# Turning the cluster codes of a routing attention: a TensorE product or a VectorE block transpose

## The chip, the cores and the metric

The kernel runs on one core of one Trainium2 chip. The metric is the device time of one execution in microseconds (us). The core has five engines that work side by side, each through its own list of instructions in order: TensorE (PE; its weight loads are shown as PEld), VectorE (DVE), ScalarE (ACT), GpSimd (POOL) and SyncE (SP). SP computes nothing here: it issues nearly all transfers between the on-chip memory (SBUF) and the device memory (DRAM), and it too works in order, so that a transfer which must wait for something holds up every transfer listed behind it.

## The reference

The first half is an attention in which a query sees only the keys of its own cluster. The second half is a two-layer feed-forward block.

```python
B, H, S, D = 4, 8, 768, 64          # 16 clusters per head
q_assign = argmax(einsum('bhsd,hcd->bhsc', q_n, c_n), -1)   # cluster of each query
k_assign = argmax(einsum('bhsd,hcd->bhsc', k_n, c_n), -1)   # cluster of each key
mask   = q_assign[:, :, :, None] == k_assign[:, :, None, :]
scores = where(mask, q @ k.T / sqrt(D), -1e9)
attn   = softmax(scores);  out = attn @ v
x = out.transpose(0, 2, 1, 3).reshape(B * S, H * D)        # 3072 x 512
h = x @ w_in                                                # 512 x 2048
y = (h - tanh(h)) @ w_out                                   # 2048 x 512
```

## The kernel before

The work is cut into 16 pairs: pair n is one batch and two heads, whose 2 x 64 dimensions fill the 128 partitions. The queries of a pair are taken in two halves of 384, and the keys in six chunks of 128. One step `(n, half, s)` treats two key chunks, so a half has three steps and there are 96 steps in all; the first batch (pairs 0 to 3) takes all its first halves first. A loop over the steps (L1238) lays down the instructions of all engines in the order in which they are to run: nothing is rearranged afterwards.

A step does this. TensorE multiplies keys and queries (`begin`, L499), ScalarE takes the exponential (L521), and VectorE multiplies it by the mask (`select`, L531). The mask is made there too: VectorE compares a row of query codes with the code of the key in its partition. TensorE then multiplies the values with the result (`value`, L556). For the first halves of pairs 1 to 3 (`masked`) the mask is instead a second TensorE product of one-hot codes that is added to the scores (L510), with the tile `hot` from which `one_hot` (L474 and L478) makes them.

The codes come from `similar` (TensorE, L376), `turn_back`, `route` and `route_on` (VectorE, L386 to L414). They end in the tile `code`, one token per partition and 24 columns per pair (two sides, two heads, six chunks). The query codes must also be had along a row, the same row in all partitions. That is what `publish` and the functions behind it do: `publish` (L425) turns the 12 columns of the query side (24 columns, both sides, for masked pairs) into 12 or 24 rows of 128 codes and stores them in DRAM as `q_codes`, a row of 256 bytes (B) from each partition. `spread` (L442) or `spread_both` (L459) reads them back into all partitions, as `row` or `hot`. The reading transfer waits until the storing one has landed. `publish(0)` and `publish(1)` stand in the opening, before the loop; those of pairs 2 and 3 run two steps after their `similar`; from pair 4 on `publish` is two steps after `route_on` and well ahead of the first use.

TensorE writes into PSUM, and most short-lived results (`pq` of `publish`, `sim`, `den`, `tally`, `h`, `o`, `pu` and `pd`) take turns in a pool `ps_f` of three buffers. A new one waits until the one three places earlier has been read.

Between the steps the feed-forward work of the batch before is laid down as filling for TensorE: `plain_items` (L730, L746) for half of the first batch, and a scheme with fewer products, one level of Strassen's method, for the rest (`up_product`, L933, and `down_product`, L1038). The combined weights for it are made once: VectorE's `made` (L831), stored to `up_factors` and `down_factors` (L795, L814), and read back piece by piece as `stream` (L853). `publish(4)` falls into the time in which they are made. VectorE meets `den` (L707) and `made` there, behind `publish` in its list.

The denominators of the softmax make a detour over DRAM of their own: `invert` and `compact` store a small tile with `back` (L659, L668), 128 partitions of 48 or 24 B, and read it back (L680, L685).

Of the kernel before, what the change touches and what calls it, by code (L numbers as in the profile page):

```python
# [30 lines left out]
F32 = mybir.dt.float32  # L31
BF16 = mybir.dt.bfloat16
# [7 lines left out]
P = 128  # L40
# [18 lines left out]
def kernel(  # L59
# [10 lines left out]
    nc = tc.nc  # L70
# [13 lines left out]
    HCH = NCH // 2  # L84
# [8 lines left out]
    const = ctx.enter_context(tc.tile_pool(name="const", bufs=1))  # L93
    dram = ctx.enter_context(tc.tile_pool(name="dram", bufs=6, space=DRAM))

    ident = const.tile([P, P], F32, name="ident")
# [9 lines left out]
    each = const.tile([P, 2 * (B * (HP - 1) - 1), 2 * TB // P], F32, name="each")  # L106
    other = const.tile([P, 2 * TB // P], F32, name="other")
    flag = const.tile([1, 1], I32, name="flag")

    out_r = out.rearrange("(b j p) m -> b j p m", p=P, j=NCH)  # L110

# [67 lines left out]
    def fast():  # L179
# [3 lines left out]
        rtp = cx.enter_context(tc.tile_pool(name="rtp", bufs=1))  # L183
# [7 lines left out]
        ps_f = cx.enter_context(tc.tile_pool(name="ps_f", bufs=3, space=PSUM))  # L191
# [38 lines left out]
        def constants():  # L230
            nc.vector.memset(inverses, 0.0)
            make_identity(nc, ident)
            nc.vector.memset(ones, 1.0 / words)
            nc.vector.memset(wholes, 0.0)

            mine_first = const.tile([P, 1], F32, name="mine_first")
            nc.vector.tensor_reduce(
                out=mine_first, in_=ident.rearrange("p (a b) -> p a b", b=D // 2)[:, :, 0], axis=AX.X,
                op=ALU.add,
            )  # L240
            nc.vector.tensor_copy(out=firsts, in_=mine_first.to_broadcast([P, D]))
            for c in range(C):
                nc.vector.memset(down[:, c : c + 1], float(C - c))

            spread_ = const.tile([P, 2, D], F32, name="spread_")
            nc.vector.memset(spread_, 0.0)
            nc.vector.tensor_copy(
                out=spread_[:, :, 0:C], in_=down.unsqueeze(1).to_broadcast([P, 2, C])
            )
            spread_ = spread_.rearrange("p a c -> p (a c)")  # L250
            nc.vector.tensor_tensor(out=spread_, in0=spread_, in1=ident, op=ALU.mult)
            nc.vector.reduce_sum(out=mine_code, in_=spread_, axis=AX.X)
# [54 lines left out]
        raw_qk, vals, turned, codes, q_codes = {}, {}, {}, {}, {}  # L307
        pairs = [(b, p) for b in range(B) for p in range(HP)]

        BL = 32  # L310
# [109 lines left out]
        def masked(n: int, half: int):  # L420


            return summed(n, half) and n > 0

        def publish(n: int):  # L425

            sides = 2 if masked(n, 0) else 1
            G = HCH * 4 * sides
            ps = ps_f.tile([G, P], F32, name="pq", tag="f")
            code = codes[n] if sides == 2 else codes[n][:, 0]  # L430
            code = code.rearrange("p a b c -> p (a b c)" if sides == 2 else "p j h -> p (j h)")
            nc.tensor.transpose(out=ps, in_=code, identity=ident)
            t = rtp.tile([G, P], BF16, name=f"qc{sides}")
            nc.vector.tensor_copy(out=t, in_=ps)
            shape = [2, HCH, 2, P] if sides == 1 else [2, sides, 2, HCH, P]
            q_codes[n] = dram.tile(shape, BF16, name=f"q_codes{sides}")
            order = "a j h p -> (a j h) p" if sides == 1 else "h i a j p -> (h i a j) p"
            nc.sync.dma_start(q_codes[n].rearrange(order), t)

        rows, hots = {}, {}  # L440

# [651 lines left out]
        def before(n: int):  # L1093


            def turns():
                turn(n, 1, nc.scalar)
                if rowwise(n):
                    turn(n, 0, nc.scalar)

            yield turns
            if n < HP:
                yield lambda: similar(n)
            else:
                yield None
            yield lambda: (turn_back(n), route(n), route_on(n))
            yield lambda: publish(n)
            if masked(n, 0):
                yield lambda: spread_both(n)
                yield lambda: one_hot(n)  # L1110
# [29 lines left out]
        for n in range(1, HP):  # L1140
            b, p = pairs[n]
# [35 lines left out]
        centroid_load()  # L1177
        load(0)
        constants()
        keep_warm(7)  # L1180
        centroid_norms()
# [15 lines left out]
        turn(1, 1, nc.scalar)  # L1197
        keep_warm(3)
        publish(0)
        load(2, (0,))  # L1200
        spread(0, 0)
# [12 lines left out]
        round_piece(rounding.pop(0))  # L1214
        begin(steps[1])
        publish(1)
        select(*steps[0][:2], 0)
        spread_both(1)
# [19 lines left out]
        for at, (n, half, s) in enumerate(steps):  # L1238
            b, p = pairs[n]
# [177 lines left out]
        for t, bound in (  # L1417
# [7 lines left out]
            out=fits, in0=inverse, scalar1=MOST_INVERSE * words, scalar2=None, op0=ALU.is_le  # L1425
        )
        nc.vector.scalar_tensor_tensor(
            out=fits, in0=inverse, scalar=words / SUM_MOST, in1=fits, op0=ALU.is_ge, op1=ALU.mult
        )
        checks = [fits, largest]  # L1430
        if words == 2:
            nc.vector.tensor_scalar(
                out=smallest, in0=smallest, scalar1=HIGH_LEAST, scalar2=None, op0=ALU.is_ge
# [198 lines left out]
```

## Time and profile before

| what | us |
|---|---|
| median of 3 runs (956.2 to 957.47) | 956.89 |
| the profiled execution | 955.51 |
| its span in the profile | 953.6 |
| TensorE busy in the span | 939.2 (98%) |
| VectorE busy | 580.3 (61%) |
| GpSimd busy | 510.5 (54%) |
| ScalarE busy | 293.5 (31%) |
| share of the chain of waits on TensorE | 89% |
| `pq` product (L432), 16 of them, each | 0.275 |
| copy of `pq` to `qc` (L434), 16 of them, each | 0.275 |

The span runs from the first to the last instruction of the profile; the time of an execution has another 1.9 us around it. "Busy" of TensorE is modelled for pipelined products, whose durations overlap: the distance from one start to the next says what a product costs, not its duration. The chain of waits follows the end of the kernel back, at each instruction to what released it. Where a table gives an idle time and a releaser, an instruction that waits for several things is put down to the last of them.

### The profile page before, as it was taken

Reading aid. Unit: us, or ns where it says so; the run is one execution under the profiler, and the core shown is the slowest. Engines: PE = TensorE matmul, PEld = TensorE weight load, DVE = VectorE, ACT = ScalarE, POOL = GpSimd, SP = SyncE. Lnnn points to the kernel's source line nnn. Section 1 sums busy time; section 2 is a strip of 40 time slices with the busy share of each in tenths; the row PEclk is TensorE's granted clock in tenths of the full one; section 3 lists DMA queues with packets and bytes.
Section 4 is the critical chain, followed back from the end, with each engine's and each line's share of the span. In section 5 each row is a group of like instructions: output and inputs, shape, how many; then the busy total and the mean of one; then the engine's idle time right before and its main releaser. Section 6 shows DMA issues by size and latency. Waiting matters only on the chain.

```text
span 953.6 us, 16953 instructions
## 1 busy us (share of the span) xinstructions
PE 939.2 (98%) x6584; PEld 469.0 (49%) x6584; DVE 580.3 (61%) x1111; ACT 293.5 (31%) x453; POOL 510.5 (54%) x364
## 2 busy tenths in 40 slices
PE   8999999999999999999999999999999999999997
PEld 5434443355653334444465665444456665445664
DVE  6647686976776678566845567766656338443011
ACT  5586564223332332323322112333331220222000
POOL 1026353456775465777785453867797343657500
PEclk9999999999999999999999999999999999999999
DMA  7767465892736645474565645557334223323331
GB/s 193 205 182 154 118 172 128 249 278 86 196 116 160 158 136 132 151 180 132 170 170 182 153 152 187 126 184 170 114 128 147 98 84 100 116 78 132 107 106 37
DMA packets 166764, 139.85 MB, mean 147 GB/s; under 512 B 116580, under 2 KB 145044, under 8 KB 163988
## 3 DMA queue, kind: packets, MB, share of 16 engines
q1 hardware_dynamic: 160292, 117.15, 44.7%
q0 software_dynamic: 6240, 21.50, 6.9%
q8 instruction: 54, 0.88, 0.4%
q14 instruction: 34, 0.28, 0.1%
q10 hardware_dynamic: 144, 0.03, 0.0%
HBM read 117.48 MB, written 21.17 MB: 145 GB/s over the span
## 4 chain that ended last, share of the span: by engine, by line
PE 89%; DVE 3%; DMA 2%; ACT 1%; issue 1%; SPq 0%; DVEq 0%; ACTq 0%
PE pu L933 26%; PE pd L1038 22%; PE sc L499 13%; PE av L556 13%; PE o L746 6%; PE h L730 4%; PE sim L376 1%; PE den L617 1%; DVE e L531 1%; DMA stream<-up_factors 1%; PE den L571 1%; DVE diff L899 1%; PE den L590 1%; DVE den L707 1%; DMA row<-q_codes 0%
## 5 line engine op out<-in xcount | busy, mean ns | idle before, releaser
L547 POOL TENSOR_TENSOR sum<-sum,e 128x768 f32<-128x768 f32 x112 | 207.2, 1850 | 99.7 <-DVE e L531 95.4
L531 DVE SCALAR_TENSOR_TENSOR e<-row,code,sc 128x384 f32<-128x384 bf16 x336 | 185.0, 608 | 78.3 <-ACT sc L521 53.2
L1038 PE MATMUL pd<-stream,G 128*64 128x256 f32 (+1 forms) x1728 | 191.4, 378 | 0.0
L521 ACT ACTIVATE sc<-sc 128x768 f32<-128x768 f32 x168 | 126.1, 789 | 191.1 <-PE sc L499 171.9
L1038 PEld LDWEIGHTS pd<-stream,G 128*64 128x64 f32 (+1 forms) x1728 | 131.3, 145 | 60.7 <-issue 5.7
L933 PE MATMUL pu<-xT,stream 128*64 128x384 f32 (+1 forms) x1024 | 159.0, 447 | 0.8 <-PE pu L933 0.4
L499 PE MATMUL sc<-t,t 64*128 64x384 f32 x768 | 149.3, 506 | 0.6 <-ACT e L521 0.3
L556 PE MATMUL av<-e,vals 128*64 128x384 f32 x768 | 145.6, 498 | 2.8 <-DVE e L531 1.6
L1002 POOL TENSOR_TENSOR G<-G,th 128x768 f32<-128x768 f32 (+1 forms) x51 | 87.1, 1723 | 69.4 <-ACT th L1000 69.2
L933 PE MATMUL pu<-diff,stream 128*64 128x384 f32 (+1 forms) x768 | 121.1, 448 | 1.8 <-DVE t L928 1.0
L933 PEld LDWEIGHTS pu<-xT,stream 128*64 128x64 f32 x1024 | 73.2, 137 | 74.7 <-issue 60.4
L499 PEld LDWEIGHTS sc<-t,t 64*128 64x128 f32 x768 | 66.7, 186 | 71.0 <-issue 34.3
L543 POOL TENSOR_TENSOR sum<-e 128x768 f32<-128x768 f32 x28 | 52.6, 1879 | 70.1 <-DVE e L531 57.2
L556 PEld LDWEIGHTS av<-e,vals 128*64 128x64 f32 x768 | 47.2, 136 | 85.0 <-issue 77.3
L1000 ACT ACTIVATE th<-G 128x768 f32<-128x768 f32 (+1 forms) x51 | 40.9, 806 | 148.9 <-DVE G L928 144.2
L746 PE MATMUL o<-w_out,g 128*64 128x512 f32 x384 | 86.1, 593 | 0.0
L933 PEld LDWEIGHTS pu<-diff,stream 128*64 128x64 f32 x768 | 53.8, 137 | 58.3 <-issue 45.4
L928 DVE TENSOR_TENSOR G<-pu,u 128x384 f32<-128x384 f32 x72 | 39.8, 552 | 32.9 <-PE pu L933 32.9
L746 PEld LDWEIGHTS o<-w_out,g 128*64 128x64 f32 x384 | 27.4, 137 | 50.1 <-issue 49.6
L1053 DVE SCALAR_TENSOR_TENSOR c<-pd,du 128x256 f32<-128x256 f32 x36 | 15.1, 419 | 48.8 <-PE pd L1038 48.8
L730 PE MATMUL h<-xT,w_in 128*64 128x384 f32 x256 | 42.8, 486 | 0.0
L1053 DVE SCALAR_TENSOR_TENSOR du<-pd,du 128x256 f32<-128x256 f32 x31 | 13.1, 423 | 48.6 <-PE pd L1038 48.1
(139 smaller groups left out, 835.2 us busy)
## 6 DMA issues: line engine op xcount, KB each, us to landing
stream<-up_factors SPq DMA_DIRECT2D x32, 896.0 KB
stream<-down_factors SPq DMA_DIRECT2D x21, 1024.0 KB
raw<-in_moe_w_in_dram POOLq DMA_DIRECT2D x16, 512.0 KB, 5.2
raw<-in_moe_w_out_dram POOLq DMA_DIRECT2D x16, 512.0 KB, 5.0
again<-in_moe_w_in_dram SPq DMA_DIRECT2D x32, 256.0 KB
again<-in_moe_w_out_dram SPq DMA_DIRECT2D x32, 256.0 KB
vals<-in_v_dram SPq DMA_DIRECT2D x32, 192.0 KB
row<-q_codes SPq DMA_DIRECT2D x29, 192.0 KB
```

The lines of the kernel that those rows point to most:

```text
L499: nc.tensor.matmul(sc[i][:, h, 0:TB], lhsT=turned[n, 1][r].rearrange("p a n -> p (a n)")[:, j * P : (j + 1) * P], rhs=turned[n, 0][r, half ...
L521: nc.scalar.activation(out=out, in_=sc[i][:, :, 0:TB], func=ACT.Exp, scale=SCALE)
L531: nc.vector.scalar_tensor_tensor(out=e[:, h].rearrange("p (j n) -> p j n", n=P), in0=rows[n, half][:, h], scalar=(codes[n][:, h, 1, j : j ...
L543: nc.gpsimd.tensor_tensor(out=s, in0=pair[0], in1=pair[1], op=ALU.add)
L547: nc.gpsimd.tensor_tensor(out=s, in0=s, in1=pair[i], op=ALU.add)
L556: nc.tensor.matmul(avs[n, half][h * D : h * D + D], lhsT=vals[n][:, h, j], rhs=e[i][:, h], start=(j == 0), stop=(j == NCH - 1),)
L730: nc.tensor.matmul(h[r], lhsT=w_in[i][:, c, o * P : (o + 1) * P][:, r], rhs=xT[c][:, half], start=(c == 0), stop=(c == CD - 1),)
L746: nc.tensor.matmul(acc[sub][r], lhsT=gs[f % HF][:, f // HF, sub * P : (sub + 1) * P][:, r], rhs=w_out[f // FQ][:, f % FQ], start=(f == seq ...
L933: nc.tensor.matmul(ps[r], lhsT=streams[base + i][:, c, k_, r], rhs=right[c], start=(c == 0), stop=(c == CH - 1),)
L1000: nc.scalar.activation(out=th, in_=t, func=ACT.Tanh)
L1002: nc.gpsimd.tensor_tensor(out=t, in0=t, in1=th, op=ALU.subtract)
L1038: nc.tensor.matmul(out_, lhsT=w, rhs=x, start=(i == 0), stop=(i == HF - 1))
```

## The change

`publish` no longer uses TensorE. VectorE copies the columns of `code` into the first columns of a 32-column bf16 tile `listed_codes`, whose rest is zero. Then it transposes that tile in blocks of 32 by 32 into `t`. A block transpose leaves the four groups of 32 tokens in four groups of partitions: partition 32 g + c holds code column c for the 32 tokens of group g. So the store writes, from each of the 128 partitions, one run of 32 codes (64 B) to its place in a DRAM tile of 32 rows of 128 codes. What readers get is a view of its first 12 or 24 rows, laid out as before. The unused rows are stored as well. The tile `t` and the DRAM tile have one name and shape for all pairs now, so that the single buffer of `t` is shared by pairs with 12 and with 24 columns. One memset of `listed_codes` joins the constants at the start.

```diff
+    listed_codes = const.tile([P, 32], BF16, name="listed_codes")
...
             nc.vector.memset(wholes, 0.0)
+            nc.vector.memset(listed_codes, 0.0)
...
             sides = 2 if masked(n, 0) else 1
             G = HCH * 4 * sides
-            ps = ps_f.tile([G, P], F32, name="pq", tag="f")
             code = codes[n] if sides == 2 else codes[n][:, 0]
             code = code.rearrange("p a b c -> p (a b c)" if sides == 2 else "p j h -> p (j h)")
-            nc.tensor.transpose(out=ps, in_=code, identity=ident)
-            t = rtp.tile([G, P], BF16, name=f"qc{sides}")
-            nc.vector.tensor_copy(out=t, in_=ps)
-            shape = [2, HCH, 2, P] if sides == 1 else [2, sides, 2, HCH, P]
-            q_codes[n] = dram.tile(shape, BF16, name=f"q_codes{sides}")
-            order = "a j h p -> (a j h) p" if sides == 1 else "h i a j p -> (h i a j) p"
-            nc.sync.dma_start(q_codes[n].rearrange(order), t)
+            nc.vector.tensor_copy(out=listed_codes[:, 0:G], in_=code)
+            t = rtp.tile([P, BL], BF16, name="qc")
+            nc.vector.transpose(out=t, in_=listed_codes)
+            kept = dram.tile([BL, P], BF16, name="q_codes")
+            nc.sync.dma_start(kept.rearrange("c (g t) -> g c t", t=BL), t)
+            if sides == 1:
+                q_codes[n] = kept[0:G].rearrange("(a j h) p -> a j h p", a=2, h=2)
+            else:
+                q_codes[n] = kept[0:G].rearrange("(h i a j) p -> h i a j p", h=2, i=sides, a=2)
```

The instruction lists of the two kernels differ in nothing else: 16 products fewer on TensorE, 16 more instructions and the memset on VectorE, 16 stores of another form at the same places in SP's list, and the waits that follow from the three-buffer turn without `pq`. ScalarE's and GpSimd's lists are the same.

## The prediction

> **What bounds the kernel now.** I read the page's busy times first, then the chain that ended last, then the instructions of the tile `pq`. From the page, busy time by engine and the chain by engine:
>
> ```profile
> PE 939.2 (98%) x6584; PEld 469.0 (49%) x6584; DVE 580.3 (61%) x1111; ACT 293.5 (31%) x453; POOL 510.5 (54%) x364
> ...
> PE 89%; DVE 3%; DMA 2%; ACT 1%; issue 1%; SPq 0%; DVEq 0%; ACTq 0%
> ```
>
> TensorE is busy nearly all the time and carries 89% of the chain, so time taken out of its list comes off the end, unless something else is late at that place. The view of the tile `pq` (durations min/median/max in ns; then who waited, us and times):
>
> ```profile
> L432 PE MATMUL pq<-ident,code x16: 273/275/281, 14.2 to 732.0; 128*12 128x128 f32 x13, 128*24 128x128 f32 x3
> L434 DVE CAST qc<-pq x16: 268/275/280, 14.5 to 732.3; 12x128 bf16<-12x128 f32 x13, 24x128 bf16<-24x128 f32 x3
> ...
>   DVE qc L434: 13.6, 8
> ```
>
> What a product costs is the step from its start to the next start, in TensorE's timeline (start, us, what):
>
> ```profile
> 34.61 0.28 PE L432 MATMUL pq<-ident,code 128*24 128x128 f32 x1
> 34.83 1.56 PE L499 MATMUL sc<-t,t 64*128 64x384 f32 x8
> ...
> 173.55 0.28 PE L432 MATMUL pq<-ident,code 128*12 128x128 f32 x1
> 173.76 3.65 PE L746 MATMUL o<-w_out,g 128*64 128x512 f32 x16
> ```
>
> The steps are 0.22 and 0.21; I use 0.21 us. VectorE meanwhile waited for the product 13.6 us in all, in 8 places.
>
> Two of TensorE's few waits matter (us in all, times, longest), from its waits:
>
> ```profile
> PE av L556 <- DVE e L531: 1.6, 1, 1.6
> ...
> PE pu L933 <- DMA stream<-up_factors: 0.3, 1, 0.3
> ```
>
> The first, at 21.1 to 22.7, is the opening: VectorE's first masks start at 22.04, when GpSimd's wait for pair 0's `row` ends. The second, at 202.17, is the first `stream` piece, at the end of the stage in which the weights are combined. A third is smaller and seen only in the chain (start, us):
>
> ```profile
> 49.78 0.23 PE pq L432
> ...
> 50.33 3.62 DMA q_codes<-qc
> ...
> 54.52 4.34 DMA hot<-q_codes
> ...
> 59.66 0.50 PE sc L510 x4
> ```
>
> The product at 58.00 is eight L499; elsewhere L510 follows such eight after 1.39 (34.83 to 36.22), here after 1.66, so TensorE lost 0.27 waiting for pair 3's `hot`.
>
> [...]
>
> **The change part by part.**
>
> TensorE loses 16 steps of 0.21, 3.4 us. The first two lie before the opening's wait, which ends by VectorE; they count only through it. The next three (pairs 2 to 4) lie before the wait at 202. Eleven lie after it: 11 x 0.21 = 2.3 us. The turn of `ps_f` without `pq` only makes later tiles wait for older ones, so I cost it at nothing.
>
> VectorE: the copy of 128x12 lies between the 0.15 of its 128x1 operations and the 0.20 of its 128x64 copy: 0.17. For the block transpose, 128x384 takes 0.593 and 128x768 0.956; the line through both gives 0.26 at 32 columns. With a gap of 0.04 that is 0.47, against 0.275 for the old copy: 0.2 x 16 = 3 us more on an engine that is 61% busy and loses 13.6 us of waits. The bound is 0.35 to 0.6 each. Nothing waits for it but the store. The memset at the start lies ahead of the weight loads; VectorE then waits elsewhere.
>
> The store: what a small piece costs is seen in SP's timeline, in two stores after each of which a dependent read is waiting:
>
> ```profile
> 225.03 0.32 SPq L438 DMA_DIRECT2D q_codes<-qc  x1
> 226.31 0.32 SPq L454 DMA_DIRECT2D row<-q_codes  x1
> ...
> 252.09 0.34 SPq L659 DMA_DIRECT2D back<-each  x1
> ...
> 253.57 1.09 SPq L680 DMA_DIRECT2D den<-back  x2
> ```
>
> `q_codes`, one piece per engine, takes 1.28 to the read; `back`, 128 pieces of 48 B, 8 per engine if 16 take part, 1.48. So 7 pieces cost 0.20, 0.028 each, and 31 more cost 0.87 us. The bounds are 0.2 (16 engines after all) and 1.7 (twice the price in a busy stage). SP waits that much longer before each read; `row` from pair 4 on is read 10 us or more ahead of its use, which hides it.
>
> Now the places where the store is on the path:
> - Opening, pair 0. VectorE has `code` at 13.69 and waits for the product until 14.47; the copy ends at 14.75. Now the pair ends at 14.2: 0.55 earlier, and the store lands 0.87 later: +0.3 (-0.4 to +1.2). TensorE stands idle there, so it starts 0.3 later.
> - Pair 3. VectorE reaches `publish` at 47.9 instead of 50.0. `hot` of pairs 1 and 2 come later by about 0.8 and 0.6, which they may: each is ready 1.2 and 3.5 us before its first L510. Pair 3's store starts about 1 us earlier net, lands about as soon as before or sooner, and the 0.27 goes: -0.3.
> - Pairs 2 to 4: -0.6 on TensorE, which so reaches 202 about 0.6 earlier than before.
> - The stage up to 202 is not TensorE's: VectorE waited 1.53 for pair 4's `pq` ahead of `den` and `made`, and SP behind them is held by DMAs (from 175 to 205 the 16 engines' mean share is 0.85 to 1.06). VectorE is about 1.3 earlier; part of it reaches the stores. On the other side four engines carry 0.87 more of small pieces. I take `stream` 0.3 earlier (-0.9 to +0.5). What TensorE gained before is then worth only those 0.3.
>
> Sum: -0.3 at 202, then -2.3: **-2.6 us**. The profiled execution (955.51: span 953.6 and 1.9 around it) would become 952.9. It lies 1.38 below the median of the runs, 956.89, which becomes **954.3**.
>
> **The rivals.**
> 1. All of it reaches the end: the store takes no longer, the opening gains 0.4, and `stream` comes early enough. That is 0.4 + 0.27 + 0.6 + 2.3 = 3.6 us: 953.3. For it speaks the small difference of the two stores above; against it the fullness of the DMA engines before 202.
> 2. The gain is given back at the two places that don't belong to TensorE: the opening +1.2, `stream` +0.5 or later. After 202 only 2.3 remain, less 0.5 to 2: 955.1 to 956.6, largely too little to tell from no change.
> 3. Slower: the 64 B writes are serial[...]. The place is the loop of pairs 1 to 3: store, `hot`, `one_hot`, the next pair's route behind it on VectorE, the next store. Three stores in a row stand before L510 at 59.66. With a price p per piece and 31 p = 3.1 (p = 0.1): `hot` of pair 1 is +3.0; pair 2's store starts +1.9 and its `hot` is +5.0; pair 3's starts +1.6 and its `hot` is +4.7. Then TensorE is late by 4.7, less 2.9 for pairs 2 to 4 and the last eleven: +1.8, 958.7. At p = 0.08 the loss and the gain are equal; that is the point from which it decides. `back` speaks against it with 0.028; for it, that `back` spread its pieces over four times as many engines.
>
> That nothing happens because the product stays is excluded: TensorE's list has 16 products fewer.
>
> **How the numbers follow.** Forecast 0.55 (own range 953.5 to 955.3), rival 1 0.15, rival 2 0.20, rival 3 0.10. About 0.2%, 1.9 us, is what a measurement of this kernel can tell from no change, so faster means below 955.0. The forecast gives 0.50 of that, rival 1 0.15, rival 2 0.03: faster 0.68. Within 0.2%: 0.05 of the forecast, 0.16 of rival 2, 0.01 of rival 3: 0.22. Slower: 0.10, nearly all rival 3. The range is 952.7 to 956.6: it takes in rivals 1 and 2 and leaves out rival 3 and the outer ends.
>
> **What would show it.** After: no L432; TensorE's busy time some 4 us less; a block transpose of about 0.26 behind a copy of about 0.17; the first mask near 22.3 (22.04 now); store to read near 2.1 in the quiet stages (1.28 now); L510 near 59 without its gap; the wait for `stream` near 202 as long or longer. I am wrong if that last wait grows by over a microsecond, if the first mask moves by over 1, or if TensorE waits for `hot`.

## The result and the profile after

| | before | after |
|---|---|---|
| median (us), 7 runs each | 956.89 (956.2 to 958.54) | 952.35 (950.19 to 954.35) |
| ratio after / before, 95% interval | | 0.995 (0.9935 to 0.9964) |
| the profiled execution: time, span | 955.51, 953.6 | 952.35, 950.5 |

The kernel after is faster by 4.5 us between the medians; the forecast was 954.3, with a range down to 952.7. The direction was right and the size too small. The same kernel measured once more (`e4_again` below) gave 953.72 and a ratio of 0.997 (0.9958 to 0.9982). By the two intervals the gain is 3.4 to 6.2 us and 1.7 to 4.0 us, so some 3 to 5 us is what can be said of the change; and two measurements of one kernel can lie 0.2% apart, which the comparisons below must bear.

The page of the kernel after, busy time by engine (share of the span, instructions) and the chain that ended last:

```profile
PE 935.3 (98%) x6568; PEld 468.2 (49%) x6568; DVE 594.2 (63%) x1128; ACT 293.0 (31%) x453; POOL 510.9 (54%) x364
...
PE 90%; DVE 4%; DMA 2%; issue 1%; ACT 1%; SPq 0%; DVEq 0%; ACTq 0%
```

TensorE's busy time fell by 3.9 us. VectorE's rose by 13.9, not by the 3 that the prediction had, and its share of the chain grew from 3% to 4%. The view of the tile `listed_codes` says why (ns min/median/max, first and last start):

```profile
L433 DVE CAST listed_codes<-code x16: 138/1029/4399, 13.5 to 728.0; 128x12 bf16<-128x12 f32 x13, 128x24 bf16<-128x24 f32 x3
L435 DVE STREAM_TRANSPOSE qc<-listed_codes x16: 211/211/214, 13.7 to 731.0; 128x32 bf16<-128x32 bf16 x16
```

The transpose is cheap, 0.21 us every time. The copy takes 0.14 to 0.18 for pairs 0 to 3, and 1 us and more in 11 of the other 12 places. TensorE's waits after (us in all, times, longest):

```profile
PE sc L502 <- DVE e L534: 1.9, 1, 1.9
...
PE av L559 <- DVE e L534: 0.9, 1, 0.9
...
PE pu L936 <- DMA stream<-up_factors: 0.4, 1, 0.4
```

The opening's wait has shrunk from 1.6 to 0.9, that for `stream` has hardly changed, and a new one of 1.9 us stands at the top. It lies near 571, and a large part of this study is about it.

**Where the time went, by place.** The table compares starts of the same TensorE groups (rows `sim` and `den`) in the profiled executions: each number is the start in that kernel less the start in the kernel before (negative is earlier). The five kernels shown start 0.25 us earlier than the kernel before at 9.3. So does h4_before_row (0.30), which has nothing of the change, so this is not the change's doing.

| start in before | what lies up to here | after | e2_products | e5_only8 | e6_to4 | h1_old12_row |
|---|---|---|---|---|---|---|
| 9.3 | the start | -0.25 | -0.26 | -0.25 | -0.25 | -0.26 |
| 26.6 | opening, wait for the first mask | -0.89 | -1.44 | -0.57 | -1.48 | -1.64 |
| 190.0 | pairs 1 to 4 | -2.11 | -1.88 | +0.64 | -2.71 | -2.86 |
| 207.9 | wait for `stream` | -1.97 | -0.81 | +1.82 | -2.70 | -2.86 |
| 351.8 | pairs 5 to 8 | -2.80 | -0.83 | +1.59 | -2.70 | -3.71 |
| 371.9 | one wait of TensorE, at 364.9 in before | -3.84 | -1.87 | +0.55 | -2.70 | -4.75 |
| 550.2 | pairs 9 to 11 | -4.92 | -1.88 | +0.54 | -2.71 | -5.83 |
| 579.0 | pair 12, the new wait | -2.15 | +1.08 | +1.06 | -1.78 | -5.88 |
| 795.0 | pairs 13 to 15 | -3.23 | +1.20 | +1.05 | -1.79 | -6.96 |

After loses 2.77 us in one place, more than half of what it has gained by then. Apart from 0.14 at `stream` nothing else is given back.

### The profile page after: what moved, and what is told of

Its sections match the earlier page's. It is cut to its first block, busy times and chain, and to the rows that moved or that the text cites. A ratio compares the mean times of both kernels' runs of the same rounds, so it can differ in the third digit from the quotient of the medians.

```text
span 950.5 us, 16935 instructions
## 1 busy us (share of the span) xinstructions
PE 935.3 (98%) x6568; PEld 468.2 (49%) x6568; DVE 594.2 (63%) x1128; ACT 293.0 (31%) x453; POOL 510.9 (54%) x364
## 4 chain that ended last, share of the span: by engine, by line
PE 90%; DVE 4%; DMA 2%; issue 1%; ACT 1%; SPq 0%; DVEq 0%; ACTq 0%
PE pu L936 26%; PE pd L1041 22%; PE sc L502 14%; PE av L559 13%; PE o L749 6%; PE h L733 4%; PE sim L378 1%; DVE e L534 1%; DVE made L834 1%; PE den L574 1%; PE den L620 1%; DMA stream<-up_factors 1%; PE den L593 1%; DMA up_factors<-made 1%; DVE den L710 1%
```

## The experiments: where the gain comes from

Every kernel in this and the next section does the whole computation. Ratios are against the kernel before, measured on the same chip in the same session. Where there is "one run", its time says little by itself (single executions of the kernel before lie between 954.5 and 960.1); such a kernel is read by its trace.

**e4_again**: the kernel after, unchanged.

> The changed kernel itself, for a second trace and more times. If the wait of 1.9 us near 572 is part of every execution, it is in this trace too and the time is 951 to 954; if it comes and goes, it is below 1 here and the span is up to 2.5 us shorter.

Measured: 953.72 us, ratio 0.997 (0.9958 to 0.9982). TensorE waits 2.7 us near 572, and by the same starts as in the table the loss there is 3.8. So the new wait belongs to the kernel and not to one execution.

**e2_products**: the kernel after with the sixteen products put back; nobody reads them.

```diff
+            ps = ps_f.tile([G, P], F32, name="pq", tag="f")
+            nc.tensor.transpose(out=ps, in_=code, identity=ident)
             nc.vector.tensor_copy(out=listed_codes[:, 0:G], in_=code)
```

> The changed kernel with the 16 TensorE products of the codes put back at their old places; nobody reads what they give, and they turn in the pool of three as before. Theory A (the gain is made of TensorE's own steps, 0.21 each and up to 0.36 with the gaps around them, and of VectorE no longer waiting for them): TensorE's share comes back, 14 x 0.21 to 14 x 0.36 = 2.9 to 5 us on TensorE up to the places where VectorE decides; VectorE's share stays, that is the earlier first mask (0.65) and no wait near 360 (0.8): the time is 1 to 2 us below the kernel before, 955 to 956. Theory B (only TensorE's steps count): all is lost and the time is that of the kernel before, 957, with the wait near 364 back.

Measured: 956.57 us, ratio 1.0001 (0.9993 to 1.0009). Its column in the table splits the gain. With the products back nothing is gained between 208 and 352, or between 372 and 550, so what after gains there (0.83 and 1.08 us) is the products. The 1.04 at 364.9 stays, so it is VectorE's. All that VectorE gave, and in this profile more, is lost again near 575, where TensorE waits 3.1 us. So the column is that of the first account up to 550, and the time that of the second.

The second surprise is the size. Pairs 5 to 8 give 0.21 each, as predicted, but pair 4 and all from pair 9 on give 0.36 (by the starts in after). TensorE's timeline of the kernel before at pair 9 (start, us):

```profile
387.63 2.75 PE L933 MATMUL pu<-xT,stream 128*64 128x384 f32 x16
390.31 0.28 PE L432 MATMUL pq<-ident,code 128*12 128x128 f32 x1
390.52 1.51 PE L933 MATMUL pu<-diff,stream 128*64 128x384 f32 x8
391.86 1.46 PE L933 MATMUL pu<-xT,stream 128*64 128x384 f32 x8
```

and the same place after:

```profile
383.79 2.75 PE L936 MATMUL pu<-xT,stream 128*64 128x384 f32 x16
386.37 1.46 PE L936 MATMUL pu<-diff,stream 128*64 128x384 f32 x8
387.66 1.46 PE L936 MATMUL pu<-xT,stream 128*64 128x384 f32 x8
```

The product's own step is 390.31 to 390.52, 0.21. But the sixteen products ahead of it take 2.68 to the next start where they take 2.58 without it, and the eight behind it 1.34 where they take 1.29. The product broke an even run of products and cost 0.15 us in its neighbours.

**e5_only8**: the kernel before with the new turn and store for pair 8 alone (`publish` chooses by `n == 8`).

> The kernel before, with the new way for pair 8 alone and the old one for the other 15. Theory A (in the kernel before VectorE waits 2.6 us for the product of pair 8, and this makes it late for the weights product 22 us later): TensorE is 0.2 ahead of the kernel before behind 342 and 0.8 to 1.1 ahead behind 365, by this one pair; its wait of 0.80 near 364 is gone. Theory B (the wait near 364 has another cause and went by chance): 0.2 ahead at both places and the wait of about 0.8 stays.

Measured: one run, 956.64 us. Its column steps by 1.04 between 352 and 372, as after's does. The lines of the kernel before show the chain: VectorE's timeline, then TensorE's wait (us in all, times, longest).

```profile
342.70 0.28 DVE L434 CAST qc<-pq 12x128 bf16<-12x128 f32 x1 [2.58 <-PE pq L432]
342.91 2.55 DVE L707 RECIPROCAL den<-den 128x128 f32<-128x128 f32 x3
```

```profile
PE pu L933 <- DVE G L928: 0.8, 1, 0.8
```

VectorE stood 2.58 us at pair 8's copy because the product lay late in TensorE's list. `den`, a mask and `made` queued behind it, and 22 us later TensorE waited 0.8 us for `G`. One pair's change removes that. (The +0.64 in its column at 190 is a wait of 1.25 us for pair 3's `hot`, to which the entry on pair 3 below returns.)

**e3_only0**: the new way for pair 0 alone (`n == 0`).

> The kernel before with the new turn and store for pair 0 alone. The prediction's account (the store's 32 pieces on each of four DMA engines land 0.87 us later, VectorE is 0.55 us earlier) gives the first masked e 0.3 us later than before, near 22.3. The account read from the kernel after (the opening's store waits in the queues behind the loads, so its pieces cost nothing, and all of VectorE's earlier start comes through, with the row's issue no longer behind the copy) gives it 0.5 to 0.7 us earlier, 21.3 to 21.5, and TensorE's wait for it 0.9 instead of 1.6 us. At the end 0 to -0.7 us of it is left: 956 to 957 us.

Measured: one run, 955.83 us. The first masks start at 20.84 (before 22.04), and TensorE's wait for them is 0.8 in place of 1.6. The sign is the second account's, and the gain even larger: at 26.6 it is 1.19, or 0.94 without the common 0.25. It loses 1.0 at `stream`, as kernels without any gain there did too (e5_only8, g2_long12), and 1.0 near 575 to the row of codes, of which the next section tells.

**e6_to4**: the new way for pairs 0 to 4 (`n <= 4`), all that lies ahead of the wait for `stream`.

> The kernel before with the new turn and store for pairs 0 to 4, those that lie ahead of TensorE's wait for the stream near 202. The prediction's account (the stream comes only 0.3 us earlier, so what is gained before is worth 0.3): TensorE waits there about 1.5 us longer than before, and from 208 on its groups start 0.3 us before those of before. The rival (the stream's transfer is issued when TensorE frees its buffer, so it moves with TensorE): they start 1.5 to 2 us earlier, and keep that to 550. Behind that the time depends on the place near 572, where VectorE's stream is six places on: 954.5 to 957 us.

Measured: one run, 953.86 us. It is 2.71 us ahead at 190 and 2.70 at 208, so the `stream` wait took nothing. Over all the profiled executions that wait is 0 to 1.2 us. It is 1.0 or more in e4_again, which loses 1.0 of its 2.5 there, but also in e5_only8 and g2_long12, which had gained nothing. So its size does not follow the gain ahead of it; e6_to4 and h1_old12_row, with the largest gains, wait 0.3.

## The experiments: where 2.8 us went

VectorE's timeline in the kernel after around pair 12's list:

```profile
559.43 1.04 DVE L433 CAST listed_codes<-code 128x12 bf16<-128x12 f32 x1
560.51 0.21 DVE L435 STREAM_TRANSPOSE qc<-listed_codes 128x32 bf16<-128x32 bf16 x1
...
568.23 0.42 DVE L1173 TENSOR_REDUCE smallest<-again 128x1 f32<-128x256 f32 x1 [0.92 <-DMA again<-in_moe_w_out_dram]
...
570.96 2.19 DVE L534 SCALAR_TENSOR_TENSOR e<-row,code,sc 128x384 f32<-128x384 bf16 x4
```

and before:

```profile
564.36 0.27 DVE L434 CAST qc<-pq 12x128 bf16<-12x128 f32 x1
...
571.83 0.42 DVE L1170 TENSOR_REDUCE smallest<-again 128x1 f32<-128x256 f32 x1 [0.31 <-DMA again<-in_moe_w_out_dram]
...
574.50 2.18 DVE L531 SCALAR_TENSOR_TENSOR e<-row,code,sc 128x384 f32<-128x384 bf16 x4
```

From the list to the first mask of pair 12 VectorE needs 11.53 us after and 10.14 before. TensorE waits for that mask, and in the kernel before it already waited 0.2 us for it, so there was no slack:

```profile
PE sc L499 <- DVE e L531: 0.2, 1, 0.2
```

(`again` is a second reading of the weights, which VectorE scans for their smallest size on the way.) What lengthened this row of work was found in three parts.

**e1_reduce**: the copy replaced by a reduction over an axis of length one.

```diff
-            nc.vector.tensor_copy(out=listed_codes[:, 0:G], in_=code)
+            nc.vector.tensor_reduce(
+                out=listed_codes[:, 0:G], in_=code.unsqueeze(2), axis=AX.X, op=ALU.max
+            )
```

> The changed kernel with one edit: the 12 or 24 code columns reach the 32-column tile by a VectorE reduction over an axis of length 1 instead of a copy; values and everything else stay. Theory A (the copy is held up by GpSimd, whose additions run beside it, and one such delay of 1.0 us makes VectorE late for the scores product at 572): the group drops from a median of 1.03 us (up to 4.40) to 0.15 to 0.25 each, VectorE's busy time falls by 12 to 14 us, TensorE's wait of 1.9 near 572 falls to 1 or less, and the kernel gets 1 to 2.5 us faster than the changed one, so 950 to 951.5. Theory B (the delay at 572 comes from the transfer that VectorE's check waits for): the group gets short all the same, the wait near 572 stays above 1.5, and the time is within 0.5 us of the changed kernel's.

Measured: 952.03 us, ratio 0.9947 (0.993 to 0.9963). The view of `listed_codes` there:

```profile
L433 DVE TENSOR_REDUCE listed_codes<-code x16: 135/156/178, 13.5 to 727.6; 128x12 bf16<-128x12 f32 x13, 128x24 bf16<-128x24 f32 x3
```

The same reading and writing takes 0.135 to 0.178 us in all 16 places, so the copy's time was not work. In the kernel after, its longest instance is this on VectorE, and beside it these two on GpSimd:

```profile
501.75 4.40 DVE L433 CAST listed_codes<-code 128x12 bf16<-128x12 f32 x1
```

```profile
501.97 2.37 POOL L1069 TENSOR_TENSOR G<-G 128x1024 f32<-128x1024 f32 x1
504.29 3.71 POOL L550 TENSOR_TENSOR sum<-sum,e 128x768 f32<-128x768 f32 x2
```

Each of the 12 copies that met an addition of GpSimd ended 0.03 to 0.04 us after the end of one, and as a reduction beside the same additions none took over 0.16. In the two longest cases (4.40 and 3.00 us) the copy outlasted two additions. So in these traces a copy beside an addition ends with it and a reduction does not wait; by what means the one holds up the other is not shown. But TensorE's wait near 571 stayed, at 2.0 us: VectorE now waits 2.05 us for the second `again` transfer. The copy alone was not the cause, as the second account had it.

**f1_pad10, f2_reduce_pad10, f3_before_pad14**: instructions of VectorE added at pair 5, of which nothing is used; ten in the kernel after, ten in e1_reduce, fourteen in the kernel before.

```diff
+    spare = const.tile([1, 1], F32, name="spare")
...
         def publish(n: int):
+            for _ in range(10 if n == 5 else 0):
+                nc.vector.memset(spare, 0.0)
```

> The kernel after, with ten writes of one number to a spare tile on VectorE after pair 5's list is due (about 0.06 us each, in a stage where VectorE is half idle): they compute nothing that is used, they only move VectorE's later instructions ten places on in its stream. Theory FETCH: in every kernel run so far whose TensorE stood still for about 2 us near 572, an 8 KB instruction fetch[...] ran at 564.6 to 567.7, just under the first of the two again transfers; in the kernel before and in the one with pair 8 alone it ran at 578 to 579. The second transfer's issue then took 0.7 to 0.8 us instead of 0.33 to 0.39, and its last packets came behind the next stream transfer's first ones, which take about 2 us each. Ten places on, the fetch comes about 6 us earlier, before the list is stored; the second wait of smallest falls from 0.9 to 1.8 us back to about 0.3, TensorE's wait for e from 2 to 2.7 us to under 0.4, and the time is 1.8 to 2.8 us under the kernel after: 949.6 to 951 us. Rival STORE: the new store of pair 12, in 128 pieces of 64 bytes, is what keeps the transfer back; then nothing changes, 952 to 954 us and the wait near 572 stays at 2 us or more.

> The same ten spare writes in the kernel whose codes are gathered by a reduction over an axis of length one (0.156 us) instead of a copy (median 1.03). By FETCH 0.3 to 0.5 us below the ten writes alone, about 949.3 to 950.5 us; by STORE about 952.

> The kernel before, TensorE's product and 256-byte store kept everywhere, with fourteen spare writes on VectorE at pair 5, which put its instructions at pair 12 at just the place in the stream that they have in the kernel after (place 946 for pair 12's list). FETCH: the fetch now runs at about 568.6, under the again transfers issued at 568.1; smallest waits 0.9 to 2.5 us for the second, TensorE about 2 us for e near 575, and the time is 1.5 to 3 us above before: 958.4 to 960 us. STORE: no new store, so no loss: 956.5 to 957.5 us.

The DMA view of the kernel after, window 564 to 566, has a line that the same view of the kernel before lacks from 564 to 577 (queue, kind: packets, MB, share):

```profile
q14 instruction: 1, 0.01, 1.7%
```

It is one 8 KB fetch of instructions. By the packets' times it ran at 564.6 in after and at 578.1 in before. Ten added instructions moved it to 559.1, fourteen moved that of before to 568.1, so it is VectorE's. Where it meets the two `again` transfers, SP's second issue is slow (start, us, both issues together), after and before:

```profile
564.13 1.24 SPq L1158 DMA_DIRECT2D again<-in_moe_w_out_dram  x2
```

```profile
568.06 0.81 SPq L1155 DMA_DIRECT2D again<-in_moe_w_out_dram  x2
```

Measured: f3_before_pad14 958.11 us, ratio 1.0014 (1.0002 to 1.0026). Moving the fetch under the transfers, with the old store, costs the kernel before about 1.3 us: VectorE waits 1.65 for the second `again` and TensorE 1.4. It is less than expected, and the interval (0.2 to 2.5 us) lies only just above zero. f1_pad10: 951.14 us, ratio 0.994 (0.9925 to 0.9955). The second wait of `smallest` fell from 0.92 to 0.24, TensorE's from 1.9 to 1.4, and the loss at pair 12 from 2.8 to 0.9; the time alone would not separate it from the first measurement of the kernel after (0.9935 to 0.9964). The fetch is a cause, but not the only one. f2_reduce_pad10: 950.68, ratio 0.993 (0.9916 to 0.9944). Copy and fetch are both out of the way there, and yet TensorE waits 2.0 us in its profile, which is that of the slowest of its six runs (952.56); VectorE names something new:

```profile
571.19 2.19 DVE L539 SCALAR_TENSOR_TENSOR e<-row,code,sc 128x384 f32<-128x384 bf16 x4 [1.58 <-DMA row<-q_codes]
```

**f4_only12**: the kernel before with the new way for pair 12 alone (`n == 12`).

> The kernel before, with the new turn and store for pair 12 alone. STORE: this store alone brings the wait, so smallest waits 0.9 to 2.5 us for the second again transfer and TensorE about 2 us near 575: 958 to 959.5 us. FETCH: VectorE's stream is two places off that of before, the fetch stays near 577 to 578, smallest waits about 0.3, TensorE 0.2 to 0.7: 956 to 957.5 us.

Measured: one run, 958.42 us. The fetch stayed at 578.0, as FETCH said, but the loss came all the same: VectorE's list step took 1.03 + 0.21 us, the second wait of `smallest` was 0.79, TensorE waited 1.8, and 2.7 were lost. So FETCH alone falls.

**g2_long12**: the kernel before with one spare instruction of 0.9 us behind pair 12's copy.

```diff
             nc.vector.tensor_copy(out=t, in_=ps)
+            if n == 12:
+                nc.vector.reciprocal(out=spare, in_=spare)
```

> The kernel before with one thing added: a reciprocal of a spare 128x128 tile on VectorE (0.9 us, its result unread) right behind pair 12's copy of the turned codes; store, product and fetch as before (VectorE's stream is two places on). SLACK: the first masked e starts about 0.9 us later, TensorE waits 1.0 to 1.2 us near 576 in place of 0.2, and the end comes 0.9 us later, or up to 2.3 if the granted clock falls after the wait as it did in four of the kernels so far: 957.6 to 959 us. Rival: VectorE has slack there and only the new store and the fetch cost time: within 0.2 us of before.

Measured: 958.33 us, ratio 1.0019 (1.0011 to 1.0028). With product, store and fetch as before, 0.9 us more of VectorE at this place costs 1.8 us (1.1 to 2.7). In its profile VectorE waits 0.40 for `row` besides, TensorE waits 1.7 in place of 0.2, and its mean granted clock is 0.997, against 1.000 in the profile of before, as in the kernel after, where the clock halves behind the wait (the last section has more on that); so the price exceeds 0.9. There is no slack, and a held-up copy of 1 us is a loss here and not, as elsewhere, free.

**g1_old12**: reduction, ten spare instructions, and pair 12 on its old product, copy and store.

> The codes gathered by a reduction of length one, ten spare writes at pair 5, and pair 12 alone kept on TensorE's product, the 0.27 us copy and the 256-byte store. Theory SLACK: in the kernel before, TensorE already waits 0.2 us near 575 for the first masked e of that pair, so VectorE's row of work ahead of it and the transfers it takes up (two again transfers, the row of codes) have no slack there; the new turn (1.0 us longer with the copy held up), the instruction fetch under the transfers, and the later store each cost their whole length. With all three gone from this pair VectorE's chain is that of before: TensorE's wait near 571 is that of before plus what TensorE itself has gained on it by then, under 1.0 us, the loss under 1 us against the 2.2 to 4.3 of the kernels so far, and the time 950 us or a little under, 0.5 to 1 us below the ten writes alone. Rival ARRIVAL: TensorE is 5 us ahead of the transfers by then, whatever this store does, and waits about 2 us anyway: 951.5 to 953 us.

Measured: 949.6 us, ratio 0.9932 (0.9918 to 0.9945). The loss was 1.24 us, between the two theories. VectorE's chain was short, but it waited for `row`, with the old store:

```profile
569.78 2.19 DVE L561 SCALAR_TENSOR_TENSOR e<-row,code,sc 128x384 f32<-128x384 bf16 x4 [1.26 <-DMA row<-q_codes]
```

The reading of `row` is issued behind the two `again` transfers and 0.5 us ahead of a `stream` piece of 896 KB. Of the first packets of that piece (7 KB each, 0.27 us as a rule) five take 1.3 to 1.8 us here. The last four kernels put it elsewhere.

**h1_old12_row, h2_pad10_row, h3_after_row, h4_before_row**: pair 12's first `row` is read right behind its store, ahead of the `again` transfers; in g1_old12, f2_reduce_pad10, after and before.

```diff
-            yield lambda: publish(n)
+            yield lambda: (publish(n), spread(n, 0) if (n, 0) in early else None)
...
-                    if not masked(*to[:2]):
+                    if not masked(*to[:2]) and to[:2] not in early:
```

> The kernel with the reduction, ten spare writes and pair 12 on its old turn and store, and pair 12's first row read issued right behind its store, ahead of the two again transfers. If the row is late because it runs into the stream transfer: it now lands near 564, VectorE has no wait for it, TensorE's wait near 570 falls from 1.4 us to under 0.5, and the time is about 1 us below that kernel's 949.6: 948.4 to 949.2. If the row is late only because TensorE has become 6 us early there and VectorE's chain is as late: TensorE's wait stays above 1 us, 949.3 to 950.3.

> The same early row with the new turn and store in all pairs (reduction, ten spare writes). The store of 64-byte pieces lands about 1 us later than the old one, still ahead of any use. With fetch, copy and row out of the way the loss near 572 is under 0.7 us, and pair 12's product is saved as well: 948 to 949 us. If the new store itself holds back the again transfers, TensorE still waits 1.5 to 2 us: 950 to 951.

> The kernel after with the early row alone: held-up copy and fetch are still there, and the row was not what ended the wait in its profile. The chain of VectorE stays about as late and TensorE still waits 1 to 2.5 us near 571: 951 to 953.5 us. If the row, or its meeting with the again transfers and the stream, was the cause all along, the loss of 2.8 us goes: 949 to 950.5.

> The kernel before with the early row alone. Its own profile lost only 0.2 us there, but kernels that are like it at this place lost about 1 us to the row (pair 0 alone turned the new way: 1.0). If that is common in its executions, its median falls by 0.3 to 1 us, to 955.6 to 956.3; if not, it stays within 0.3 us.

SP's timeline of h1_old12_row, with the row ahead of the rest:

```profile
558.83 0.33 SPq L468 DMA_DIRECT2D q_codes<-qc  x1
560.11 0.34 SPq L485 DMA_DIRECT2D row<-q_codes  x1
562.23 0.81 SPq L1186 DMA_DIRECT2D again<-in_moe_w_out_dram  x2
563.13 0.38 SPq L884 DMA_DIRECT2D stream<-up_factors  x1
```

| kernel | us | ratio, interval | lost from 550 to 579, by the starts |
|---|---|---|---|
| h1_old12_row | 949.28 | 0.9932 (0.9918 to 0.9945) | 0.0 |
| h2_pad10_row | 949.63 | 0.993 (0.9916 to 0.9943) | 0.0 |
| h3_after_row | 950.59 | 0.9942 (0.9929 to 0.9955) | 1.1 |
| h4_before_row | 955.88 | 0.9991 (0.9983 to 0.9999) | 0.0 |

With row, copy and fetch out of the way next to nothing is lost in these profiles, whichever store pair 12 has (in h2_pad10_row a wait of 0.6 us takes up the 0.36 that pair 12's product would have given): the store of 64-byte pieces was not the cause. h3_after_row still has the held-up copy (1.03) and loses 1.1. The fetch still lies at 565.0 there, but both `again` issues are over by 565.12 (0.81 us in place of 1.24), and the second transfer is waited for 0.59 instead of 0.92. So most of the 1.1 is likely the copy's; no run has the early row and the fetch without the copy. In the kernel before the early row is worth about 0.9 us of the median (0.1 to 1.6), though the profile of before shows a wait of only 0.2: other executions of it probably lose more there, as e3_only0, e5_only8 and e6_to4 do (0.5 to 1.0, with VectorE waiting for `row`).

The times do not show the row's part when copy and fetch are gone: g1_old12 and h1_old12_row have one ratio, 0.9932, and f2_reduce_pad10 and h2_pad10_row another, 0.993. There it rests on single profiles. These four are the best kernels and can't be told apart, 5 to 8 us under the kernel before by their intervals.

## Why the prediction was right or wrong

Three steps of the prediction failed above all: VectorE's longer list was costed at nothing, the gain ahead of `stream` was held to be worth only 0.3, and the change in one profile was carried over to the median unchanged. Up to 208 the sum had -0.3, and the profile has -1.97 (0.25 of it the common start). Behind 208 the sum had -2.3, and the profile has -1.26 up to 795: -2.99 by the products of ten pairs, -1.04 at 364.9, +2.77 at pair 12. The totals, -2.6 and some -3.2, are near each other by luck: these misses cancel. By its own steps:

- **TensorE's products: right, mis-sized.** "11 x 0.21 = 2.3 us" behind 202 counted the product's own step. Four pairs gave 0.21, but from pair 9 on, and at pair 4, a product cost 0.36, because the groups around it also ran closer without it.
- **Pair 3: right in this profile.** L510 (now L513) follows its eight products after 1.39 us without the gap, and the start behind it moves by 0.28 (predicted 0.3):

```profile
56.69 1.56 PE L502 MATMUL sc<-t,t 64*128 64x384 f32 x8
58.08 0.49 PE L513 MATMUL sc<-hot 64*128 64x384 bf16 x4
```

  But that gap is not fixed. In the five other kernels that keep the old way for pairs 0 to 3 it is nothing (f4_only12, g2_long12), 0.2 (f3_before_pad14), 1.2 (e5_only8) and 2.3 us (h4_before_row); in the eleven that turn all of these pairs the new way it is nothing. The longest:

```profile
61.36 0.50 PE L511 MATMUL sc<-hot 64*128 64x384 bf16 x4 [2.28 <-DVE hot L479]
```

- **The store: right in size where it is quiet, and only there.** The store to its dependent read takes 1.94 and 2.39 (223.41 and 261.50) where the kernel before had 1.28 and 1.29: 0.7 to 1.1 more, predicted 0.87. The counts of pieces per engine behind the 0.87 (1, 8 and 32) fit the packets of the traces: the old store at 225.03 is 12 packets of 256 B with 12 of 4 B, `back` at 252.09 is 128 of 48 B with 16 of 4 B, and the new store at 223.41 is 128 of 64 B with 4 of 4 B, its pieces four abreast from 224.59 to 224.86, most of them 7 ns behind the one ahead. If the packets of 4 B are the ends of the parts, there were 12, 16 and 4 parts. For pairs 1 to 3, with loads beside it, it took 3.18, 1.57 and 3.69 before and 1.96, 2.60 and 3.38 after: the price does not show.
- **The opening: wrong sign.** "+0.3" added VectorE's -0.55 and the store's +0.87. SP's timeline after, and before:

```profile
13.94 0.65 SPq L437 DMA_DIRECT2D q_codes<-qc  x1
14.64 1.74 SPq L335 DMA_DIRECT2D x<-in_q_dram  x2
16.53 0.43 SPq L457 DMA_DIRECT2D row<-q_codes  x1
```

```profile
14.78 0.38 SPq L438 DMA_DIRECT2D q_codes<-qc  x1
15.20 1.68 SPq L333 DMA_DIRECT2D x<-in_q_dram  x2
17.58 0.34 SPq L454 DMA_DIRECT2D row<-q_codes  x1
```

  Between store and read SP issues two loads of `x`. After, the read follows the end of that issuing by 0.15, and the store by 2.59; before, it followed them by 0.70 and 2.80. So there was no +0.87 here: the read came no later behind the new store, and the earlier start came through. The first mask is at 21.14, 0.9 earlier, with the common 0.25 in it. Over the profiled executions it lies at 20.4 to 21.4 in the twelve kernels that turn pair 0 the new way, and at 21.5 to 22.05 in the six that do not. That part of SP's list was in the timeline of before, and I did not lay the store beside it.
- **The stage up to 202: wrong.** "What TensorE gained before is then worth only those 0.3." Nearly all of it passes: 1.97 of 2.11 in after, 2.70 of 2.71 in e6_to4; e4_again lost 1.0 of 2.5, as kernels without any gain did. A wait for a transfer in one profile did not fix the time of the transfer when everything ahead of it moved.
- **VectorE costed at nothing: wrong twice.** "Nothing waits for it but the store" held for the next instruction and not for the queue behind it. The wait of 2.58 at pair 8 was on TensorE's path 22 us later: a gain of 1.04 missed. And 0.2 us more per pair (really 1.0, the copy being held up by GpSimd) was on the path at pair 12, where the first mask had no slack.
- **The turn of `ps_f`, the rivals.** No wait in the trace points to the shared buffers. Rival 3, serial writes of 64 B, did not happen: the reads of `hot` are issued 0.9 to 3.4 us earlier than before, and the 0.7 to 1.1 above make 0.02 to 0.04 for each of the 31 pieces, an estimate with the prediction's own count, where it needed 0.08; the packets themselves are mostly 0.007 apart. Rival 1 came nearest, 953.3: it had the opening's gain and all that lies ahead of `stream` reach the end, but neither the gain at 364.9 nor the loss at pair 12.
- **The last step, from profile to median: wrong.** The two profiled executions lie 3.2 us apart, near the 2.6 of the sum. But the prediction then added 1.38 us because the profiled execution of before lay that far under its median; the profiled execution of after lies on its median. So 1.4 of the 1.95 us by which the forecast missed come from this step. The likely reason is that the one profile of before met short waits at three places that cost more in other executions of kernels like it: `hot` of pair 3 (0.3 there, up to 2.3), `stream` (0.3, up to 1.2) and pair 12's row. The row was tested (h4_before_row); for the other two it is seen and not tested, so how the 1.4 divide stays open. In the eleven profiles with the new way the first of these waits is gone, a gain that the one profile of before shows only as 0.3.

## What to carry to other kernels

An instruction hidden behind idle time is paid for where the queue behind it next meets the bounding engine: follow that queue to every such meeting, ask how much slack each has, and look for slack of 0.2 us in particular (at pair 12 0.9 us more on VectorE cost 1.8, in g2_long12). When two waits end close together, taking one away shows the next; in the profiles here copy, fetch and row had to go together before nothing was lost at pair 12. A wait in one profile can be one draw of many: look at it in several executions before it enters a sum. On VectorE beside a busy GpSimd the small gather of this kernel was better written as a reduction (0.135 to 0.178 us) than as a copy (0.37 to 4.40).

## What the runs showed of the hardware

- A cast of 128x12 or 128x24 numbers took 0.14 to 0.18 us where GpSimd added nothing beside it (pairs 0 to 3 in the kernel after); of 128x12 it took 0.37 to 4.40 us, mostly over 1.0, beside GpSimd's additions. As a reduction the two took 0.135 to 0.178 everywhere (e1_reduce).
- Ten and fourteen small instructions added to VectorE at pair 5 moved an 8 KB fetch of instructions near pair 12 by 5.5 and 10 us; where it came to lie under transfers (f3_before_pad14) the kernel was 1.3 us slower (0.2 to 2.5).
- After the wait near 571 TensorE's granted clock halved, in the kernel after from 572.8 to 576.2. Windows of the kernel after (stretch and its length in us; busy share and count of TensorE, its weight loads, VectorE, ScalarE and GpSimd; then the clock, DMA share, GB/s):

```profile
571.00:572.00 1.00, 0.00 (x0) 0.00 (x0) 1.00 (x2) 0.00 (x0) 0.00 (x0) 1.00 1.03 428
...
573.00:574.00 1.00, 1.00 (x4) 0.53 (x4) 0.89 (x3) 0.50 (x1) 0.70 (x1) 0.50 0.87 338
574.00:575.00 1.00, 1.00 (x6) 0.12 (x4) 0.02 (x1) 0.30 (x1) 1.00 (x1) 0.50 0.22 84
```

  The loss at pair 12 was about 1 us more than the wait (2.8 against 1.9 in after, 3.8 against 2.7 in e4_again). By the mean granted clock of the profiled executions, 0.997 in six kernels and 0.998 or more in the others, the drop followed waits of 1.7 to 2.7 us in those six and none of up to 1.4 us, but not the 1.7 of h3_after_row or the 3.1 of e2_products, nor the 2.3 near 60 of h4_before_row. So the length of the wait alone does not decide it here; what does, no run shows.
